# An attention and gMLP kernel: 16 of the 40 probability-times-V products of each last-segment iteration moved behind the second logits, and the last output product narrowed to 128 columns

## The chip, the cores and the metric

The kernel runs on one core of one Trainium2 chip. The metric is the device time of one execution in microseconds (us). Below, PE is the TensorE matmul engine (PEld its weight loads), ACT is ScalarE, DVE is VectorE, POOL is GpSimd, and SP is the engine whose queue issues all DMA transfers. PE writes its results to PSUM, a memory divided into banks; to evacuate a result is to read it from there with another engine. PV stands for the products of the probabilities with V. A store has landed when its transfer is reported complete. The hole is the time from the end of one round of logits to the earliest start of the next, which has to wait for an exponential.

## The reference, cut to what matters

```python
# A: attention with a memory, over 4 segments of 512 tokens, 32 heads of width 32
for s in range(N):
    logits = einsum('bhqd,bhkd->bhqk', qs, ks) * scale + mask     # causal within the segment
    p = softmax(logits); a_dot = einsum('bhqk,bhkd->bhqd', p, vs)
    a_mem = (phi(qs) @ M) / (phi(qs) @ z + 1e-06)
    o = g * a_mem + (1 - g) * a_dot
    M = M + phi(ks)^T vs;  z = z + sum(phi(ks))                   # not needed after the last segment
h = x + o @ wo
# B: gMLP on layernorm(h): gelu(h w_in), a 2048x2048 token mixing, then @ w_out, added to h
```

`M` and `z` are the memory. Nobody reads their update of the last segment, so the kernel leaves it out. That is why the last segment differs from the others.

## The kernel before

The attention works in 32 iterations `n` (4 segments `s` x 8 groups `c` of four heads). Each has three rounds of logits, all into the same four PSUM banks. ACT takes the exponential of each round, and the next round may overwrite the banks only after that. Projections for the next iteration (`qk`), PV products of the previous one and the state update stand between the rounds:

```python
    def pv(n):
        c = n % NQ
        for cq in range(4):                      # query block
            for j in range(cq + 1):              # key blocks up to it: 4+8+12+16 = 40 matmuls in all
                rnd, o = {...}[j]
                for i in range(4):
                    pe.matmul(PVA[:, cq, i, :], E[n % 2][rnd][:, i, o:o + 128], V[:, j, 4 * c + i, 0:33], ...)
        norm(n)                                  # DVE: 4 instructions

    def state(n):
        if s == NSEG - 1:
            return
        # ... 4 matmuls PK x V -> PSUM, then DVE: MSUM[:, c] += ..., MZB[:, c, :, 0:33] = MSUM * mask

    # main loop, n = 0 .. 31
        logits(n, 0)
        fill(f1)                                 # k projection of n + 1: 8 matmuls of 512 columns
        if n > 0:
            pv(n - 1)
        logits(n, 1)
        if n > 0:
            state(n - 1)
        bg_pop()
        fill(f2)                                 # q projection of n + 1
        logits(n, 2)                             # from segment 1 on with mem(n), which reads MZB[:, c]
        # ... fill(f3), fill(f4): V or output projections
```

The end of the kernel, one pass per row block `tc` (cut):

```python
            sp.dma_start(fin[:], out2d[tc * 128:(tc + 1) * 128, :])
            for lo, w in ((0, 512), (512, 512)) if tc < NTC - 1 else ((0, 512), (512, 256), (768, 256)):
                b = next_bank()
                hs = slice(lo, lo + w)
                mm8(PS[:, b, 0:w], lambda i: YT[...], lambda i: WOUT[:, i, hs], n=14)
                dve.tensor_tensor(fin[:, hs], fin[:, hs], PS[:, b, 0:w], ALU.add)
                sp.dma_start(out2d[tc * 128:(tc + 1) * 128, hs], fin[:, hs])
```

The softmax here doesn't subtract the row's maximum and nothing guards it: scores larger than these inputs give would overflow.

## Time and profile before

| | before |
|---|---|
| time, median of the first 3 runs | 802.81 us (802.80 to 803.01) |
| span of the profiled execution | 2199.8 us |
| mean granted clock of that execution | 1.000 |

The profiled execution took 2.7 times as long as the timed ones, although the granted clock reads 1.00. Why it was so slow is not shown. It may be used for durations on ACT, DVE and POOL, but not for how long PE waits. From the profile page of before come the span and each engine's busy time with its share of the span:

```profile
span 2199.8 us, 12431 instructions
PE 2168.2 (99%) x5304; PEld 694.2 (32%) x5374; DVE 384.4 (17%) x777; ACT 304.6 (14%) x348; POOL 122.3 (6%) x239
```

The timeline of one last-segment iteration of the same slow profile follows. Its columns are start, duration, engine, source line, operation, output<-input, shape, count, and in brackets the idle time before with what ended it:

```profile
768.23 0.67 PE L209 MATMUL ps<-qk_114 32*128 32x384 bf16 x8
768.96 1.88 ACT L209 ACTIVATE e_123<-ps 128x2048 bf16<-128x2048 f32 x1 [1.70 <-PE ps L209]
769.23 4.38 PE L209 MATMUL ps<-xnT_82,wq 128*128 128x512 bf16 x7 [0.32 <-issue]
...
773.53 0.45 PE L209 MATMUL ps<-qk_114 32*128 32x256 bf16 x4
```

The second logits are followed by their exponential on ACT, 1.88 us. Meanwhile PE runs the q projection, so slowly here (over 4 us) that the third logits at 773.53 never wait. In a timed run PE is about three times as fast, and a wait can exist there that this profile cannot show.

### The profile page before, as it was taken

How to read it: one execution, taken by the hardware profiler on the slowest of the kernel's cores; microseconds unless marked ns; L12 is line 12 of the kernel's file. 1: busy time of each engine (PE TensorE's matmuls, PEld its weight loads, DVE VectorE, ACT ScalarE, POOL GpSimd, SP SyncE). 2: the span in 40 equal slices, each digit the busy share in tenths (PEclk: the TensorE clock that was granted, in tenths of full speed). 3: DMA queues.
4: the chain of work that ended last, by engine and by line, in shares of the span. 5: the costliest groups of instructions: out<-in, count | busy, mean ns of one | idle time of the engine just before them, and what ended most of it. 6: DMA issues, size and time to landing. Idle time of an engine off the chain costs nothing.

```text
span 2199.8 us, 12431 instructions
## 1 busy us (share of the span) xinstructions
PE 2168.2 (99%) x5304; PEld 694.2 (32%) x5374; DVE 384.4 (17%) x777; ACT 304.6 (14%) x348; POOL 122.3 (6%) x239
## 2 busy tenths in 40 slices
PE   9999999999999999999999999999999999999999
PEld 3233332333333333333332222222222222222223
DVE  2221113322321232211220000011011101101110
ACT  2222222233233332011111111000000000000000
POOL 1111001111111110000110000000000000000000
DMA  4110111211201102100002000400120030000001
GB/s 153 27 48 15 29 24 25 53 22 37 51 20 46 41 20 60 39 17 19 19 19 48 0 0 0 112 0 0 31 48 0 12 67 0 0 22 20 0 2 31
DMA packets 125000, 64.79 MB, mean 29 GB/s; under 512 B 94864, under 2 KB 113936, under 8 KB 124944
## 3 DMA queue, kind: packets, MB, share of 16 engines
q1 hardware_dynamic: 124944, 63.99, 11.6%
q8 instruction: 42, 0.69, 0.1%
q14 instruction: 14, 0.11, 0.0%
HBM read 32.51 MB, written 8.39 MB: 19 GB/s over the span
## 4 chain that ended last, share of the span: by engine, by line
PE 99%; issue 1%; DVE 0%
PE ps L209 99%; DVE msum L209 0%; DVE etmp L209 0%; DVE fin_150 L209 0%; DVE ident L209 0%
## 5 line engine op out<-in xcount | busy, mean ns | idle before, releaser
L209 PE MATMUL ps<-w_out,yT 128*128 128x512 bf16 (+1 forms) x453 | 264.9, 818 | 2.9 <-issue 2.9
L209 PE MATMUL ps<-wspT_139,z_137 128*128 128x512 bf16 x439 | 264.2, 836 | 3.2 <-issue 3.2
L209 PE MATMUL ps<-wspT_140,z_137 128*128 128x512 bf16 x439 | 263.9, 836 | 3.3 <-issue 3.3
L209 PE MATMUL ps<-wo,oT 128*128 128x512 bf16 x254 | 162.5, 869 | 0.9 <-issue 0.9
L209 PEld LDWEIGHTS ps<-w_out,yT 128*128 128x128 bf16 x462 | 81.2, 176 | 186.2 <-issue 183.1
L209 PEld LDWEIGHTS ps<-wspT_139,z_137 128*128 128x128 bf16 x448 | 78.8, 176 | 188.0 <-issue 188.0
L209 PEld LDWEIGHTS ps<-wspT_140,z_137 128*128 128x128 bf16 x448 | 78.7, 176 | 188.0 <-issue 188.0
L209 PE MATMUL ps<-xnT_81,wk 128*128 128x512 bf16 x128 | 92.1, 946 | 0.0
L209 PE MATMUL ps<-xnT_81,wq 128*128 128x512 bf16 x114 | 85.2, 966 | 5.7 <-DVE msum L209 3.1
L209 PE MATMUL ps<-xnT_82,wk 128*128 128x512 bf16 x128 | 88.0, 915 | 0.0
L209 PE MATMUL ps<-xnT_82,wq 128*128 128x512 bf16 x112 | 79.7, 933 | 7.0 <-issue 7.0
L209 PEld LDWEIGHTS ps<-wo,oT 128*128 128x128 bf16 x256 | 45.7, 180 | 102.2 <-issue 102.0
L209 DVE TENSOR_TENSOR tmpg_146<-ps,brow_144 128x512 f32<-128x512 f32 x14 | 9.7, 692 | 380.4 <-DMA brow_144<-in_B_b_sp_dram 274.2
L209 ACT ACTIVATE z_137<-ps 128x448 bf16<-128x448 f32 x60 | 32.6, 544 | 253.5 <-PE ps L209 253.5
L209 DVE BATCH_NORM_STATS2 zst<-z_137 128x6 f32<-128x448 bf16 x64 | 39.2, 622 | 153.6 <-ACT z_137 L209 153.6
L209 ACT ACTIVATE z1T<-ps 128x512 bf16<-128x512 f32 x56 | 33.4, 597 | 233.3 <-PE ps L209 233.3
L209 DVE RECIPROCAL rd<-ps 128x16 f32<-128x16 f32 x32 | 8.2, 258 | 253.8 <-PE ps L209 253.8
L209 PE MATMUL ps<-wv_83,xnT_81 128*128 128x512 bf16 x62 | 45.5, 960 | 1.0 <-issue 1.0
L209 PE MATMUL ps<-wv_84,xnT_82 128*128 128x512 bf16 x64 | 46.2, 971 | 0.0
L209 PE MATMUL ps<-wv_84,xnT_81 128*128 128x512 bf16 x64 | 46.0, 953 | 0.0
L209 PE MATMUL ps<-wv_83,xnT_82 128*128 128x512 bf16 x64 | 45.9, 951 | 0.0
L209 PEld LDWEIGHTS ps<-xnT_81,wq 128*128 128x128 bf16 x128 | 24.4, 195 | 51.1 <-issue 50.7
(266 smaller groups left out, 1887.7 us busy)
## 6 DMA issues: line engine op xcount, KB each, us to landing
w_out<-in_B_w_out_dram SPq DMA_DIRECT2D x1, 3584.0 KB, 13.3
wo<-in_A_wo_dram SPq DMA_DIRECT2D x1, 2048.0 KB, 8.9
xr_88<-in_A_x_dram SPq DMA_DIRECT2D x8, 256.0 KB, 2.9
xr_89<-in_A_x_dram SPq DMA_DIRECT2D x8, 256.0 KB, 2.9
win_134<-in_B_w_in_dram SPq DMA_DIRECT2D x2, 896.0 KB, 5.0
wk<-in_A_wk_dram SPq DMA_DIRECT2D x1, 1536.0 KB, 8.8
wq<-in_A_wq_dram SPq DMA_DIRECT2D x1, 1536.0 KB, 12.5
out_dram<-hch_90 SPq DMA_DIRECT2D x6, 256.0 KB, 2.1
```

Of the source, the lines that this page charges most:

```text
L209: ins = getattr(e, op.name)(*op.args, **op.kw)
```

## The change

Two independent edits. In the last segment, the fourth query block of `pv` (16 of 40 matmuls), and the normalization after it, move behind the second logits, to give PE more work while ACT computes that exponential. The last row block's output products become 512 + 384 + 128 columns, so that less is left to evacuate and store after the last matmul.

```diff
-    def pv(n):
+    def pv(n, cqs=range(4)):
         c = n % NQ
-        for cq in range(4):
+        for cq in cqs:
             ...
-        norm(n)
+        if 3 in cqs:
+            norm(n)
@@ main loop
         if n > 0:
-            pv(n - 1)
+            pv(n - 1, range(3) if s == NSEG - 1 else range(4))
         logits(n, 1)
+        if s == NSEG - 1:
+            pv(n - 1, (3,))
         if n > 0:
             state(n - 1)
@@ end
-            ... else ((0, 512), (512, 256), (768, 256)):
+            ... else ((0, 512), (512, 384), (896, 128)):
```

More of the change, by code (lines that the diff above doesn't have):

```diff
@@ L875, in bass_sequential_preLN__memory_aug_infini_attn__mixer_gmlp__prompt_kernel @@
             sp.dma_start(fin[:], out2d[tc * 128:(tc + 1) * 128, :])
-            for lo, w in ((0, 512), (512, 512)) if tc < NTC - 1 else ((0, 512), (512, 256), (768, 256)):
+            for lo, w in ((0, 512), (512, 512)) if tc < NTC - 1 else ((0, 512), (512, 384), (896, 128)):
                 b = next_bank()
```

## The prediction

> **What bounds the kernel.** TensorE. The page's busy table gives PE 99% of the span, DVE 17%, ACT 14%; the chain of waits is 99% PE. But this profile is not the timed program: its span is 2199.8 us against 802.81 us timed, although the granted clock reads 1.00. In its timeline, 512-column matmuls of the last segment follow each other every 0.62 us. The Trainium skill ("TensorE: Matmul & The Clock Gate", "Wait, 56ns, not 53.3ns?") gives 215.7 ns at full clock; this trace does not show that rate, but the timed total needs it: about 3264 full-width equivalents (counted from the kernel) x 215.7 ns = 704 us, an estimate, leaves some 98 us for logits, PV, state, start and tail. ACT and DVE durations can be read from the trace; PE waits are hidden in it, because PE is 3 times too slow to wait. I rebuild them.
>
> **What the change does.** In the 8 iterations of the last segment it moves 16 of the 40 small PV matmuls (and the norm after them, DVE: 0.26+0.18+0.69+0.69 us) from before the second logits to after them. The last row block's two 256-column products become 384 and 128.
>
> **Cost of the wait it fills.** The second logits (PE) -> exp of 128x2048 on ACT (1.877 us, groups view) -> third logits, which overwrite the same PSUM banks. In the timeline ACT starts 0.06 us after the logits end; with the return, the hole is about 2.0 to 2.1 us. Before, only one q projection stands in it in this segment (no state update): 8 x 0.2157 = 1.73 us at full clock. PE so waits about 0.3 to 0.4 us per iteration (estimate). The PV pairs run at about 43 ns even in this slow trace (40 in 1.7 us), so 16 are 0.5 to 0.7 us: they fill the hole. The hole after the first logits keeps k projection 1.73 + 24 PV about 0.85 to 1.0 = 2.6 us or more, over 2.1, so no new wait opens, except perhaps in the first two iterations, where a V copy (0.6 us on ACT) delays that exp. Gain: 8 x 0.35 = 2.8 us, all on the critical path: PE is the limit, ACT has about 6.6 us of work in an iteration of some 9 us.
>
> **Risk of the move.** The norm comes later on DVE, ahead of the memory norm, which must free the logits banks, and of the WO evacuation (0.69 us), which must free one of only two projection banks. I estimate some 0.4 us of slack there; part of the gain can be lost.
>
> **Tail.** The last evacuation shrinks from 0.42 us (256 columns) to about 0.29 us (0.69 at 512 and 0.42 at 256 give 1.05 ns a column). The SP issue, about 0.35 us, fits between. Gain 0.1 to 0.2 us.
>
> **Predicted time:** 802.81 - 2.8 - 0.1 = 799.9 us; 8 in 10 between 798.3 and 802.2. Faster by over 2%: 0.01; within 2%: 0.98; slower by over 2%: 0.01.
>
> **What would show it.** If a profile at full clock comes: PE idle before the third logits, released by ACT's exp, about 0 in the last segment, but 0.3 to 0.4 us there in a full-clock profile of the kernel before; no idle at the second logits; norm starting after the third stretch of PV; the final evacuation near 0.29 us. In a slow profile only the order shows.
>
> **What would make it wrong.** The hole is smaller (full-clock PV or projections slower than I think) and the gain under 1 us; the shorter cover makes the second logits wait; DVE's later norm delays bank releases; or the final 128-column product is bound by weight loads.

## More of the kernel before

Every operation goes through a recorder, which derives semaphore waits from the memory cells that operations touch.

```python
        if kind == "dram":
            gran = 1024                 # bytes per cell
        else:
            gran = GRAN if kind == "sbuf" else 2048     # GRAN = 32 bytes; PSUM: a bank
        # ... cells lo // gran to hi // gran; a write waits for the last writer of each of its cells
```

## The result, and the profile after

The ratios are fast runs against the fast runs of the other kernel in the same rounds. They are not quite the ratios of the medians quoted beside them, and differ from ratios of the plain means by up to 0.0002.

| | before | after |
|---|---|---|
| median, first comparison (4 runs each) | 802.91 us | 802.18 us |
| ratio, 95% interval | | 0.9991 (0.9973 to 1.0008) |
| ratio, second set of rounds | | 0.9986 (0.9973 to 0.9998) |
| ratio, third set of rounds | | 0.9990 (0.9977 to 1.0002) |

The time is the same within 2%, and just inside the predicted range, by 0.02 us. The gain is 0.7 to 1.1 us where 2.9 us had been predicted. The profile after is of a fast execution. From its page:

```profile
span 800.9 us, 12431 instructions
PE 790.9 (99%) x5304; PEld 380.8 (48%) x5374; DVE 380.5 (48%) x777; ACT 298.6 (37%) x348; POOL 127.3 (16%) x239
```

ACT and DVE are busy for nearly the same microseconds as in the slow profile. PE differs by far, and so the share of the span that everything else has. PE is still the limit.

Here is the timeline of one last-segment iteration after the change, the lines that answer to those of before:

```profile
274.63 0.40 PE L209 MATMUL ps<-qk 32*128 32x384 bf16 x8
274.96 0.57 PE L209 MATMUL ps<-v,e 128*128 128x33 bf16 x16
275.08 1.88 ACT L209 ACTIVATE e<-ps 128x2048 bf16<-128x2048 f32 x1 [0.34 <-PE ps L209]
275.59 1.67 PE L209 MATMUL ps<-xnT,wq 128*128 128x512 bf16 x7
...
277.19 0.29 PE L209 MATMUL ps<-qk 32*128 32x256 bf16 x4
```

The 16 moved products stand from 274.96 to about 275.37. The q projection follows. Its first matmul record is missing (7 of 8), so it starts near 275.37. The third logits start at 277.19 without a wait. The exponential had ended at 276.96.

### The profile page after: what moved, and what is told of

It is laid out like the page before. It is cut to its first block, busy times and chain, and to the rows that moved or that the text cites. A ratio compares the mean times of both kernels' runs of the same rounds, so it can differ in the third digit from the quotient of the medians.

```text
span 800.9 us, 12431 instructions
## 1 busy us (share of the span) xinstructions
PE 790.9 (99%) x5304; PEld 380.8 (48%) x5374; DVE 380.5 (48%) x777; ACT 298.6 (37%) x348; POOL 127.3 (16%) x239
## 4 chain that ended last, share of the span: by engine, by line
PE 95%; DVE 4%; issue 1%; ACT 0%
PE ps L209 95%; DVE stats L209 1%; DVE maskg L209 0%; DVE ta L209 0%; DVE otok L209 0%; DVE hch L209 0%; DVE pqk L209 0%; ACT e L209 0%; DVE rd L209 0%; DVE lno L209 0%; DVE etmp L209 0%; DVE qk L209 0%; DVE mzb L209 0%; DVE rdm L209 0%; DVE msum L209 0%
## 5 line engine op out<-in xcount | busy, mean ns | idle before, releaser
L209 PE MATMUL ps<-wspT,z 128*128 128x512 bf16 x878 | 193.1, 379 | 0.9
L209 ACT ACTIVATE e<-ps 128x2048 bf16<-128x2048 f32 (+1 forms) x96 | 152.8, 1592 | 49.3 <-PE ps L209 48.8
L209 PEld LDWEIGHTS ps<-wspT,z 128*128 128x128 bf16 x896 | 87.7, 98 | 105.7
L209 POOL TENSOR_SCALAR_AFFINE_SELECT e<-e 128x512 bf16<-128x512 bf16 x128 | 84.4, 671 | 185.4 <-ACT e L209 185.4
L209 PE MATMUL ps<-win,hnT 128*128 128x448 bf16 x512 | 98.3, 352 | 0.0
L209 PE MATMUL ps<-w_out,yT 128*128 128x512 bf16 (+2 forms) x453 | 96.9, 372 | 0.5
L209 PE MATMUL ps<-hnT,win 128*128 128x512 bf16 x439 | 96.2, 379 | 0.5
L209 PE MATMUL ps<-xnT,wk 128*128 128x512 bf16 x256 | 60.8, 380 | 0.0
L209 PE MATMUL ps<-wv,xnT 128*128 128x512 bf16 x254 | 58.7, 379 | 0.2 <-issue 0.2
L209 PE MATMUL ps<-wo,oT 128*128 128x512 bf16 x254 | 57.6, 379 | 0.1
```

The lines of the kernel that those rows point to most:

```text
L209: ins = getattr(e, op.name)(*op.args, **op.kw)
```

## The experiments

All outputs are right. Chip and rounds are shared within each table.

### First set: a full-clock profile of before, and the two edits apart

The kernel before was run unchanged, for its profile.

> The kernel before, unchanged, for a profile at full clock (its first profile was nearly 3 times too slow). Theory A (the hole was smaller than I thought): the third logits of the last segment start 0.05 to 0.15 us after the end of the q projection, so the 8 iterations held only about 1 us of waiting, and an iteration with an output projection takes about 9.4 us against 9.33 us in the changed kernel. Theory B (the hole was 0.3 to 0.4 us as predicted, but something gave the gain back): the third logits wait 0.3 us or more per iteration, an iteration takes 9.6 to 9.7 us, and the stretch from the first to the last logits of the segment is over 2 us longer than in the changed kernel. Span 800.5 to 801.5 us if the profile is at full clock.

The edits alone were taken straight from the diff: `split_only` keeps the old tail `((0, 512), (512, 256), (768, 256))`, and `tail_only` keeps the old `pv` and takes the new tail.

> Only the move of 16 PV products; the tail stays 512/256/256. Theory A: 0.5 to 0.9 us faster than before, nearly all of what the whole change gave. Theory B with the loss in the tail: about 2.5 us faster than before.

> Only the 512/384/128 tail. My predicted 0.1 to 0.2 us faster; theory B with the loss in the tail: over 1 us slower than before. Within 0.3 us of before if the tail is nothing.

> The whole change again, on the same chip as its parts: 0.5 to 1.0 us faster than before; the sum of its two parts within 0.3 us.

| kernel | median, us | ratio to before (95%) |
|---|---|---|
| before (9 runs) | 803.45 | |
| before again, one run, for its profile | 804.26 | |
| split only | 801.36 | 0.9975 (0.9962 to 0.9989) |
| tail only | 804.00 | 1.0006 (0.9994 to 1.0019) |
| whole change | 802.42 | 0.9986 (0.9973 to 0.9998) |

The split alone is about 2 us faster than before, and the new tail costs it about 1 us again (802.42 against 801.36). Their intervals overlap; the third set repeats the difference (802.47 against 801.24), and the traces below show where it arises. So neither of the two theories was right as stated. The wait in the hole was smaller than thought, which A says, and part of the gain was lost in the tail, which B says. Two expectations were missed: the tail alone was 0.5 us slower (means), where a small gain, nothing or over 1 us had been expected, and the parts add up to -1.5 us against -1.15 us for the whole, just outside the 0.3 us allowed.

**The hole, read from the full-clock profile of before.** The timeline of one last-segment iteration of the unchanged kernel, now of an execution at full speed:

```profile
265.75 1.16 PE L209 MATMUL ps<-v,e 128*128 128x33 bf16 x40
266.84 0.40 PE L209 MATMUL ps<-qk 32*128 32x384 bf16 x8
267.17 1.90 PE L209 MATMUL ps<-xnT,wq 128*128 128x512 bf16 x8
267.29 1.88 ACT L209 ACTIVATE e<-ps 128x2048 bf16<-128x2048 f32 x1 [0.74 <-PE ps L209]
...
269.22 0.29 PE L209 MATMUL ps<-qk 32*128 32x256 bf16 x4 [0.15 <-ACT e L209]
```

Here the wait is visible: the third logits idle 0.15 us by the profile, released by ACT's exponential. The modelled end of the projection overlaps the true gap, so iteration lengths are the better measure. The first logits of iterations 25 and 31, and the PV products that follow the loop, in the kernel before:

```profile
244.59 0.39 PE L209 MATMUL ps<-qk 32*128 32x512 bf16 x4
301.48 0.39 PE L209 MATMUL ps<-qk 32*128 32x512 bf16 x4
310.29 1.16 PE L209 MATMUL ps<-v,e 128*128 128x33 bf16 x40
```

The same three of the changed kernel:

```profile
243.89 0.39 PE L209 MATMUL ps<-qk 32*128 32x512 bf16 x4
299.46 0.40 PE L209 MATMUL ps<-qk 32*128 32x512 bf16 x4
307.87 1.16 PE L209 MATMUL ps<-v,e 128*128 128x33 bf16 x40
```

From one iteration's first logits to the next, n = 25 to 30 take 9.48 us on average before (244.59 to 301.48 us, six iterations) and 9.26 us after (243.89 to 299.46 us). The difference is 0.22 us each, 1.32 us in six. The last iteration (n = 31, counted to the start of the PV products that follow the loop) goes from 8.81 to 8.41 us, and the first (n = 24) stays at 9.57 us. That makes 1.7 us in all.

**The tail, read from the same two kernels.** The timelines of the end of before: the last evacuations (DVE) and the transfers of the last row block (SPq lines).

```profile
798.36 0.42 DVE L209 TENSOR_TENSOR fin<-fin,ps 128x256 bf16<-128x256 bf16 x1
798.81 0.42 SPq L209 DMA_DIRECT2D out_dram<-fin  x1
799.88 0.42 DVE L209 TENSOR_TENSOR fin<-fin,ps 128x256 bf16<-128x256 bf16 x1 [1.11 <-PE ps L209]
800.51 0.33 SPq L209 DMA_DIRECT2D out_dram<-fin  x1
```

The same of the changed kernel:

```profile
796.69 0.56 DVE L209 TENSOR_TENSOR fin<-fin,ps 128x384 bf16<-128x384 bf16 x1 [0.64 <-PE ps L209]
797.27 0.33 SPq L209 DMA_DIRECT2D out_dram<-fin  x1
797.47 0.29 DVE L209 TENSOR_TENSOR fin<-fin,ps 128x128 bf16<-128x128 bf16 x1 [0.23 <-PE ps L209]
798.96 0.33 SPq L209 DMA_DIRECT2D out_dram<-fin  x1
```

And what the SP queue of the changed kernel waited for in the last 5 us (columns: who waited for whom, us in total, times, longest):

```profile
SPq L208 <- DMA out_dram<-fin: 1.3, 1, 1.3
```

Before, the last transfer is issued 0.21 us after its evacuation ends (799.88 + 0.42 = 800.30). After the change, the evacuation ends at 797.76, and the issue stands at 798.96, 1.2 us later. In between SP waits for an earlier store to the output to land. The 384-column store was issued at 797.27, and this store took 1.6 us to land (the profile's DMA view), so it landed at about 798.9.

In the kernel before, the same view has the same line with 1.2 us.

The cause is in the recorder. A DRAM cell has 1024 bytes, and a row of the output has 2048. Columns 512 to 1023 of a row are one cell. The last two stores write different columns of the same cells, so the recorder makes the last wait for the one before it. This wait is not needed. It stood in the kernel before too, but there it ended about 0.2 us after the data were ready: the store of the first 256 columns was issued at 798.81, over 1.4 us before the last evacuation ended. The new split issues the second-last store only 0.5 us before the last evacuation ends, which exposes the landing.

Counted from the PV products of the last iteration (310.29 us before, 307.87 after), the last issue comes 490.22 us later before and 491.09 us later after, so the tail lost 0.87 us. The distance repeats well: it is 491.07 to 491.10 us in all four traces of kernels with the new tail as it is, and 490.14 to 490.22 us in all five at full clock with the old tail and the same 1024-byte rule. Together with the 1.7 us of the split, that leaves a net gain of 0.8 us, which is what the times show.

### Second set: is it the needless wait, and is it the cover?

`a_fine` is the changed kernel with this edit, and `b_fine` is the kernel before with the same edit:

```diff
-            gran = 1024
+            gran = 256
```

`a_reorder` is the changed kernel with the pieces in another order:

```diff
-            ... else ((0, 512), (512, 384), (896, 128)):
+            ... else ((512, 384), (0, 512), (896, 128)):
```

`all_after` moves all 40 PV products, with the tail as before:

```diff
-            pv(n - 1, range(3) if s == NSEG - 1 else range(4))
+            if s < NSEG - 1:
+                pv(n - 1)
         logits(n, 1)
         if s == NSEG - 1:
-            pv(n - 1, (3,))
+            pv(n - 1)
```

> The changed kernel, but the recorder that places the waits tells DRAM addresses apart by 256 bytes instead of 1024, so that the last output transfer no longer waits for the one before it to land. Theory C (the tail lost its time by that needless wait: in the changed kernel the last issue stands at 798.78 us, 1.2 us after its evacuation ended): the last issue follows its evacuation within about 0.15 us, the kernel is 0.9 to 1.2 us faster than the changed one, that is 2.0 to 2.4 us faster than before. Rival D (rows of 256 bytes, or three issues close together, make the last transfer slow in itself): no faster than the changed kernel, or under 0.4 us.

> The changed kernel with the 384-column product computed first, then the 512, then the 128; the wait rule is left at 1024 bytes. The last transfer still waits for the 384-column one, but that landed long before. Theory C: as fast as with the finer rule, within 0.3 us. Rival D: no faster than the changed kernel.

> The kernel before with the finer rule. Its last evacuation ended at 800.30 us and its last issue stood at 800.51 us, so the needless wait ended about when the data were ready: theory C expects 0 to 0.2 us of gain. If the rule cost more than that also before, over 0.5 us.

> In the last segment all 40 PV products behind the second logits, tail as before. If the gain is cover for a hole of about 1.96 us after each logits (theory A in its measured form), then the first hole is now covered by 1.73 us alone and PE waits about 0.22 us before the second logits in each iteration, 0.4 us in the last: the segment's iterations last 9.55 us again and the time is within 0.6 us of before, about 2 us slower than the split alone. If the later place of PV itself is what helps (for instance by releasing the norm at a better moment), it is at least 1.5 us faster than before.

| kernel | median, us | ratio to before (95%) |
|---|---|---|
| before (9 runs) | 803.05 | |
| changed, finer rule | 801.30 | 0.9976 (0.9964 to 0.9989) |
| changed, pieces reordered | 801.37 | 0.9977 (0.9965 to 0.9990) |
| before, finer rule | 803.09 | 0.9998 (0.9984 to 1.0011) |
| all PV behind the second logits | 804.00 | 1.0009 (0.9996 to 1.0021) |

**Theory C holds.** Both ways of taking away the needless wait, one by a finer rule and one by letting the conflicting store land early, give about 1.8 us over before (2.0 to 2.4 us had been expected of the finer rule). The end of the changed kernel with the finer rule, its last two evacuations and stores:

```profile
796.20 0.55 DVE L209 TENSOR_TENSOR fin<-fin,ps 128x384 bf16<-128x384 bf16 x1 [0.70 <-PE ps L209]
796.78 0.33 SPq L209 DMA_DIRECT2D out_dram<-fin  x1
796.98 0.29 DVE L209 TENSOR_TENSOR fin<-fin,ps 128x128 bf16<-128x128 bf16 x1 [0.23 <-PE ps L209]
797.29 0.33 SPq L209 DMA_DIRECT2D out_dram<-fin  x1
```

The last store is issued 0.02 us after its evacuation. Rival D fell. The Trainium skill ("DMA: Bandwidth & Descriptors", Specifications) says that transfers below 512 bytes are read, modified and written. The narrow store has rows of 256 bytes, yet from its issue to the end of the span it took 1.9 us here, against 2.0 us for the 512-byte rows of before. By the DMA view it landed after 1.4 us, against 1.6 us for the stores of 512-byte rows, which carry twice the bytes. No run here shows such a penalty. In the kernel before, the finer rule gave nothing that the times resolve, as expected. Its wait was nearly hidden. The end of that kernel with the finer rule:

```profile
799.08 0.42 DVE L209 TENSOR_TENSOR fin<-fin,ps 128x256 bf16<-128x256 bf16 x1 [1.11 <-PE ps L209]
799.53 0.33 SPq L209 DMA_DIRECT2D out_dram<-fin  x1
```

The issue now follows the evacuation after 0.03 us instead of 0.21 us. It stands 490.04 us after the last PV products (309.49) instead of 490.22 us, so the needless wait had cost about 0.2 us before too.

**The cover.** With all 40 products behind the second logits, the wait moved to the second logits. One iteration of that kernel:

```profile
262.83 0.39 PE L209 MATMUL ps<-qk 32*128 32x512 bf16 x4
263.16 1.90 PE L209 MATMUL ps<-xnT,wk 128*128 128x512 bf16 x8
265.21 0.40 PE L209 MATMUL ps<-qk 32*128 32x384 bf16 x8 [0.15 <-ACT e L209]
265.54 1.17 PE L209 MATMUL ps<-v,e 128*128 128x33 bf16 x40
```

The 0.15 us of idle time is the same, one round of logits earlier. So it is the cover that counts and not the later place of PV. The size was missed: I had expected at most 0.6 us slower than before, and it was 0.8 us slower (means of the rounds). The trace shows where. The iterations with an output projection take 9.56 us, as expected. Iterations 25 and 26 take 9.70 us, and iteration 24, which had no wait before, now takes 9.94 us instead of 9.57 us. In these three, a V copy on ACT delays the first exponential. Iteration 25:

```profile
243.43 0.39 PE L209 MATMUL ps<-qk 32*128 32x512 bf16 x4
243.53 0.60 ACT L209 ACTIVATE v<-ps 128x512 bf16<-128x512 f32 x1 [1.13 <-PE ps L209]
244.03 1.87 ACT L209 ACTIVATE e<-ps 128x2048 bf16<-128x2048 f32 x1
245.95 0.40 PE L209 MATMUL ps<-qk 32*128 32x384 bf16 x8 [0.30 <-ACT e L209]
```

The exponential starts 0.60 us after the logits, against 0.45 us in iteration 27 (262.83 to 263.28), and the second logits idle 0.30 us instead of 0.15 us. From the first logits of n = 24 to the PV products after the loop, this kernel takes 76.07 us and the kernel before 75.27 us: the whole 0.8 us.

### Third set: the split in all segments, and the candidates side by side

`split_everywhere` drops the condition on the segment, with the tail as before:

```diff
-            pv(n - 1, range(3) if s == NSEG - 1 else range(4))
+            pv(n - 1, range(3))
         logits(n, 1)
-        if s == NSEG - 1:
+        if n > 0:
             pv(n - 1, (3,))
```

`split_again`, `fine_again` and `a0_third` are the split alone, the whole change with the finer rule, and the whole change as it is, once more.

> The split of PV in all four segments, tail as before. Theory A: in segments 0 to 2 the state update (0.25 us) already stands with the q projection behind the second logits and covers the hole of 1.96 us, so an iteration of segments 1 and 2 stays at 9.57 us and the time is that of the split in the last segment alone within 0.4 us. If the split helped by anything other than covering that hole (fewer PE bubbles, an earlier free bank), its 23 further iterations would give about 0.2 us each, over 4 us.

> The split alone again, beside the other candidates on one chip: 1.7 to 2.1 us faster than before, and as fast as the whole change with the finer rule within 0.3 us.

> The whole change with the finer rule again, the candidate for the best version: 1.7 to 2.2 us faster than before, 0.8 to 1.2 us faster than the changed kernel of the same rounds. Its traces put its last issue 0.27 us nearer to the end of the attention than the split alone; whether that shows in the time is open.

> The changed kernel as it is, beside the candidates: 0.7 to 1.1 us faster than before, about 1 us slower than the split alone.

| kernel | median, us | ratio to before (95%) |
|---|---|---|
| before (9 runs) | 803.23 | |
| split in all segments | 805.64 | 1.0031 (1.0019 to 1.0044) |
| split in the last segment | 801.24 | 0.9978 (0.9965 to 0.9990) |
| whole change, finer rule | 801.24 | 0.9978 (0.9964 to 0.9991) |
| whole change | 802.47 | 0.9990 (0.9977 to 1.0002) |

The split in all segments was a miss. I had expected it to change nothing in the earlier segments. It was 4.4 us slower than the split in the last segment alone. The 16 iterations of segments 1 and 2 take 157.65 us instead of 153.54 us, which is nearly all of it. In a trace of it, an odd iteration of segment 1:

```profile
134.47 0.69 DVE L209 TENSOR_TENSOR otok<-ta,tm 128x512 bf16<-128x512 f32 x1
135.08 0.28 DVE L209 TENSOR_TENSOR msum<-msum,ps 128x132 f32<-128x132 f32 x1
135.11 0.29 PE L209 MATMUL ps<-qk 32*128 32x256 bf16 x4
135.40 0.41 DVE L209 TENSOR_TENSOR mzb<-msum,maskg 128x132 bf16<-128x132 f32 x1
135.86 0.41 PE L209 MATMUL ps<-mzb,pqk 128*128 128x132 bf16 x4 [0.47 <-DVE mzb L209]
```

The later norm stands ahead of the state update on DVE. The memory product on PE then waits 0.47 us for that update. From 30 to 230 us, the weight loads of PE wait 4.8 us for it in all, against 0.9 us with the split in the last segment alone: 3.9 us more, nearly the whole loss of 4.1 us in these segments. Only the odd iterations show it: iteration 13 takes 10.11 us, and iterations 12 and 14 take 9.57 us. The product of group c reads `MZB[:, c]`, and the update writes `MZB[:, c - 1]`, so the data do not ask for this wait. One group of MZB has 4 x 34 x 2 = 272 bytes, which is 8.5 cells of 32 bytes, so an odd group shares its first cell with the one before it. That would be the same kind of needless wait as in the tail. It is argued from the code and the trace; no run with a padded MZB tested it.

Among the candidates, the split alone and the whole change with the finer rule tie at 801.24 us. Both are about 2 us faster than before and 1.2 us faster than the change. By the traces, the narrow last product with the finer rule issues its last store 0.27 us sooner after the attention than the split alone (489.91 against 490.18 us), of which 0.13 us is due to the narrow product (489.91 against 490.04 us with the finer rule alone). The times cannot resolve that.

## Why the prediction was right or wrong

The range held by 0.02 us, and that is luck: the medians of the same kernel in the later rounds, 802.42 and 802.47 us, lie above its end. The point was 2.3 us too low, and it was the sum of two terms that both came out too good: the gain of the split was mis-sized, and the gain of the tail was a loss.

- **What bounds the kernel: right.** PE is busy for 99% of the span in the full-clock profiles too. The rate that was taken from the Trainium skill ("TensorE: Matmul & The Clock Gate", "Wait, 56ns, not 53.3ns?") holds. In the changed kernel's trace, 408 matmuls of 448 columns took 77.34 us, 189.6 ns each, and the page's rule gives 448 / 2.4 + 2.5 = 189.2 ns, an estimate.
- **The mechanism of the split: right, its size too large.** The exponential took 1.88 us; the Trainium skill ("ScalarE: Activation LUTs", "What ACT_TABLE_LOAD costs") gives 186 ns + 0.833 ns per column for an ACTIVATE with immediate scale and bias, which makes 1.89 us for 2048 columns, an estimate that agrees. "PE so waits about 0.3 to 0.4 us per iteration" was 0.22 us. The hole itself was as predicted, 2.05 us (267.17 to 269.22). The projection covers 1.73 us of it, and the rest would be 0.32 us. But in an iteration without a wait, the third logits also start 0.09 us after the projection's 1.73 us (277.19 against 275.37 + 1.73 in the changed kernel). That step is paid in any case, and the prediction had counted it as gain.
- **"8 x 0.35 = 2.8 us": mis-sized.** The count was wrong as well as the size. In the segment's first iteration, the state update of the previous segment still stands in the hole, so there was nothing to gain: 9.57 us with and without. The last iteration gained 0.4 us, because there a 448-column projection covers less. The sum is 6 x 0.22 + 0.4 = 1.7 us by the trace, and about 2 us by the times.
- **The cost of the moved products: near.** 16 took 0.41 us (0.5 to 0.7 predicted), and the 24 that stayed left no new wait before the second logits.
- **The DVE risk: did not happen in the last segment.** Every one of its iterations with two projections and an output projection takes 9.33 us. It did happen, by another path, in the other segments when the split was tried there.
- **The tail: this step failed.** "The SP issue, about 0.35 us, fits between. Gain 0.1 to 0.2 us." The evacuation did shrink to 0.29 us as predicted, and the issue did take 0.33 us. What was left out is that the last store had to wait for the landing of the store before it. The runs showed a loss of 0.87 us in place of a gain of 0.1 us. With the wait removed, the last issue comes 0.31 us earlier than before (489.91 against 490.22 us). The kernel before gains 0.18 us of that by the same removal (one trace), so the narrow product itself is worth about 0.13 us, as predicted. The idea was sound; what failed is that the store could go out as soon as its data were ready.

The sum of the measured terms is -1.7 + 0.87 = -0.8 us, against -0.7 to -1.1 us in the times.

## What to carry to other kernels

When a product or a store is cut into smaller pieces, list what each piece waits for as the dependency tracker sees it: pieces that fall into one tracking cell are chained, and a chained store waits until its neighbour has landed (1.6 us after issue here; 1.2 us of that was exposed) when that neighbour is issued late. Work moved to cover a wait is worth only the uncovered remainder in those iterations that had one, so count them one by one from an execution at full clock. The same move in iterations without that wait has nothing to gain and can cost: here it cost 4 us.

## What the Trainium skill lacked or had wrong

- "TensorE: Matmul & The Clock Gate" ("LDWEIGHTS (loading the stationary operand)" and "Weight-path perf modes") gives a weight load as about P / 1.2 ns, which is 107 ns for 128 columns (an estimate), and about twice as fast with the fast weight load. The PV products load new 128-column weights for every matmul of 33 columns, and 40 such pairs take 1.09 us (265.75 to 266.84), 27 ns a pair. That agrees with the page's floor of about 25 ns per matmul ("Wait, 56ns, not 53.3ns?"). A load of half of 107 ns, an estimate from the page, would not fit into 27 ns, so the page's load time does not bound such a stream of pairs here.
- The same page ("Seeing it yourself") says that clock events can be unreliable and that a clock stuck at a quarter was seen for 50 us and more. Here a whole profiled execution of 2199.8 us ran PE nearly three times too slowly (a 512-column matmul every 0.62 us, against 0.22 us at full clock) while the granted clock read 1.00. The page does not warn that a whole profile can be so, nor that such a profile hides waits of PE like the 0.15 us that the full-clock profile shows. Whether the two effects are the same is not shown.
- "DMA: Bandwidth & Descriptors" ("Anatomy of one DMA") gives a fixed cost of about 2.0 us for the software path. The profile counts the transfers here as hardware ones, and for small stores they stay under that figure: from issue to landing, the traces show 1.4 to 1.7 us for stores of 32 to 128 KB.
